# A state-space scan gated by an MLP on one core: 63 tasks in other places of a hand-kept order, 13 small operations on other engines, and the last product kept in PSUM

## The chip, the core and the metric

The kernel runs on one core of one Trainium2 chip. The core has five engines with a queue each, which run in order and wait for one another by semaphores: PE (TensorE, matrix products into PSUM), ACT (ScalarE), DVE (VectorE), POOL (GpSimd) and SP (SyncE, which here issues most of the DMAs). The metric is the device time of one execution in microseconds (us); lower is better. A profile of one execution, with every instruction's start and duration, goes with it.

## The reference

One sequence of 2048 tokens with 448 channels. The normalised input goes through a diagonal complex recurrence (448 states) and, beside it, through an MLP of 1792 hidden units; the product of both is added to the input.

```python
x = A_x
xn = _layernorm(x)
# A: s
Lam_bar = exp(dt * Lam);  B_bar = ((Lam_bar - 1.0) / Lam)[:, None] * Bmat
h_t = Lam_bar * h_{t-1} + B_bar @ xn_t            # for t in 0..2047
s = 2.0 * (h @ Cmat.T).real + xn * Dskip
# B: g
y = _layernorm(xn)
g = silu(gelu(y @ w1 + b1) @ w2 + b2)
return x + s * g
```

## The kernel before

The 2048 tokens are cut into four groups (g = 0 to 3) of 512. A group has two blocks (b) of 128 partitions, and each partition holds two neighbouring tokens (par = 0, 1), so that the recurrence runs over 256 pairs of tokens.

For each group PE does four kinds of work. The first MLP product (`mm1_run`, L801) runs in 14 half-depth tiles that are handled in pairs: the 448 input channels are split over the upper and lower 64 rows of the array, so each pair has a first half (6 matmuls) and a second half (8 matmuls) that ends the sums in two PSUM banks. Behind each second half ACT takes the two banks through a gelu (L805) into `gT`, which frees the banks for a later pair. The second MLP product (`mm2`, L828) has one block of 14 matmuls for each block and parity, into bank 5 or 6; DVE adds the bias and frees the bank (L831, tile o), and ACT, or ACT and DVE together, makes the silu. The products with B (`bu`, L729) go into bank 4 and are copied to `u_sb` in bf16 (L417, by ACT or DVE). The products with C (`ym`, L871, L874, L877) read the states `h_sb`.

Between `bu` and `ym` lies the recurrence (`ssm`). DVE rotates `u_sb` (L744 to L748), scans (L753, L755), ACT rounds the scan's result to bf16 (L417 vs<-s_w, in a copy of 128x1536 and a smaller one in three parts), and DVE rotates back to `h_sb` (L771 to L775).

Once, in the first 70 us, the kernel also makes its tables: the rotations W by sines on ACT (L640) from an angle whose absolute value is taken at L630/L631; the columns of parameters `cw` by many 128x4 operations (L561, L564, L592 and others, each on POOL or DVE); and the matrices CQ, CZ and LB, each row block by a scaled copy into `tmp` (L658 on ACT or L659 on DVE) and a multiply and add on DVE (L661). `M0` is four sums of seven matmuls (L712, the last one L697) with a diagonal added by DVE (L718).

What sets the order: every operation is recorded as a numbered task with what it reads and writes. At the end the tasks are given out in the order of a table of 633 numbers, `ORDER`, and each engine runs its own in that order. A second table, `SECOND`, lists the tasks that run on the second of two engines allowed for them (`small` is POOL or DVE, `copy` ACT or DVE, `combine` ACT or DVE). Waits are added where a task needs another engine's result.

The end of the program is the last `ym` of group 3, cut in columns 0 to 255 and 256 to 447. DVE multiplies each with g (L885) into `t3` in SBUF, the second operation of each (L891, on POOL for the first part and on DVE for the second) adds x, and the result is stored by DMA.

Of the kernel before, what the change touches and what calls it, by code (L numbers as in the profile page):

```python
# [8 lines left out]
ALU = mybir.AluOpType  # L9
# [150 lines left out]


ORDER = [int(k) for k in """
# [17 lines left out]
""".split()]  # L180
SECOND = [int(k) for k in """
45 53 54 61 63 66 69 74 76 83 112 130 133 158 160 162 163 165 177 184 185 187 189 190 220 222 224 226 228 230 238 248 249 258 266 268 331 362 364 365
384 400 401 436 447 468 480 482 487 491 499 501 502 504 510 528 529 609 612 627
""".split()]


# [14 lines left out]
def bass_recurrent_scan__ssm_conv_s5__mixer_channel_mlp__prompt_kernel(  # L201
# [12 lines left out]
    L, D, F = 2048, 448, 1792  # L214
# [5 lines left out]
    with ExitStack() as es:  # L220
# [27 lines left out]
        o_sb = tmp.bitcast(BF)  # L248
# [27 lines left out]
        g_sb = SB("g_sb", [128, 8, D])  # L276
        t3 = SB("t3", [128, 2, D])
# [15 lines left out]
        def dve(fn, reads=(), writes=(), dur=0.2, prio=0):  # L293
            kb.add("dve", fn, reads, writes, dur=dur, lat=0.12, prio=prio)
# [10 lines left out]
        with nc.Block():  # L305
# [513 lines left out]
            def silu_now(g):  # L819
                return bool(9 >> g & 1)  # L820
# [18 lines left out]
            def late(n):  # L839
                return n >= 15  # L840
# [17 lines left out]
            def ym(g, b, par, prio):  # L858
                gx, hb = g % 2, g % 2
                n = (2 * g + b) * 2 + par  # L860
                gs, fb, ob = n % 8, n % 2, b
                k0 = b * 128 + 1 + par
                cm = (CZ, CQ)[par]
                xs = slice(b * 128, (b + 1) * 128)
                off = (2 * g + b) * 256 * D
                last = g == NG - 1 and b == 1

                def part(c0, c1):
                    bk = 7 if g < NG - 1 else (7, 4, 0)[(2 * b + par + (c0 > 0)) % 3]
                    w = c1 - c0  # L870
                    fns = [lambda e, k=k: e.matmul(psum[:, bk, c0:c1], h_sb[:, hb, k, k0:k0 + 128], cm[:, k, c0:c1], start=(k == 0), stop=False)  # L871
                           for k in range(7)]
                    if par == 0:
                        fns += [lambda e, d=d: e.matmul(psum[:, bk, c0:c1], xnT[:, gx, d, xs], M0[:, d, c0:c1], start=False, stop=(d == 3)) for d in range(4)]  # L874
                        du, rk = 2.1, [f"M0{d}" for d in range(4)] + [f"M0{d}d" for d in range(3)] + [f"CZ{k}" for k in range(7)]
                    else:
                        fns[-1] = lambda e: e.matmul(psum[:, bk, c0:c1], h_sb[:, hb, 6, k0:k0 + 128], cm[:, 6, c0:c1], start=False, stop=True)  # L877
                        du, rk = 1.36 * w / D + (0.05 if w < D else 0), [f"CQ{k}" for k in range(7)]
                    pe(fns, [f"h{hb}", f"hh{hb}", f"hp{hb}"] + ([f"xnT{gx}_{b}"] if par == 0 else []) + rk, [f"ps{bk}"], du, prio + c0 / 1e4)
                    y, ky = psum[:, bk, c0:c1], f"ps{bk}"  # L880
                    if par and not late(n):
                        y, ky = xr[:, b, c0:c1], f"xr{b}"
                        dve(lambda e: e.tensor_tensor(xr[:, b, c0:c1], psum[:, bk, c0:c1], xd[:, g % 2 * 2 + b, c0:c1], ALU.add), [f"ps{bk}", f"xd{g % 2 * 2 + b}"] + ([f"CZ{k}" for k in range(7)] if g == 0 else []), [ky])  # L883
                    if silu_now(g):
                        dve(lambda e: e.scalar_tensor_tensor(out=t3[:, fb, c0:c1], in0=y, scalar=2.0, in1=g_sb[:, gs, c0:c1],  # L885
                                                             op0=ALU.mult, op1=ALU.mult), [ky, f"g{gs}"], [f"t3{fb}_{c0}"])
                    else:
                        dve(lambda e: e.tensor_tensor(t3[:, fb, c0:c1], y, g_sb[:, gs, c0:c1], ALU.mult), [ky, f"g{gs}"], [f"t3{fb}_{c0}"])  # L888
                    far = par and late(n)
                    res = xr[:, b, c0:c1] if far else x_all[:, 2 * g + b, par, c0:c1]  # L890
                    add = lambda e: e.tensor_tensor(o_sb[:, ob, par * D + c0:par * D + c1], t3[:, fb, c0:c1], res, ALU.add)  # L891
                    rd = [f"t3{fb}_{c0}", f"t3{fb}_256"] if c0 == 0 and not (last and par) else [f"t3{fb}_{c0}"]
                    rd += [f"xr{b}"] if far else xk(2 * g + b)
                    on = [("dve", add, 0.1 + (0.28, 0.47)[par] * w / D, 0.12), ("pool", add, 0.2 + 1.1 * w / D, 0.15)]
                    if last and par or 1:
                        kb.either(*on, rd, [f"o{ob}_{par}_{c0}"], prio)
                    else:
                        dve(add, rd, [f"o{ob}_{par}_{c0}"], on[0][2], prio)
                    if last:
                        kb.dma("act" if c0 else "sp", dram_ap(out, off + par * D + c0, [[2 * D, 128], [1, w]]), o_sb[:, ob, par * D + c0:par * D + c1], reads=[f"o{ob}_{par}_{c0}"],  # L900
                               writes=[f"out{g}{b}{par}{c0}"], prio=prio, nbytes=256 * w)
                for c0, c1 in ((0, 256), (256, D)) if last and par else ((0, D),):
                    part(c0, c1)
                if par and not last:
                    kb.dma("sp", dram_ap(out, off, [[2 * D, 128], [D, 2], [1, D]]), o_sb[:, ob, :].rearrange("p (r d) -> p r d", r=2),
                           reads=[f"o{ob}_0_0", f"o{ob}_1_0", f"o{ob}_1_256"], writes=[f"out{g}{b}"], prio=prio, nbytes=229376)
# [58 lines left out]
            for step in STEPS.split():  # L965
                k, g, a = step[0], int(step[1]), step[2:]
# [54 lines left out]
```

## Time and profile before

| | before |
|---|---|
| median of 3 runs (lowest to highest) | 153.15 us (153.08 to 153.63) |
| span of the profiled execution | 151.8 us |
| instructions | 2974 |
| DVE busy | 127.6 us (84%) |
| ACT busy | 99.0 us (65%) |
| matmuls | 1127 |
| DMA, HBM read and written | 6.89 MB, 1.84 MB |

The span runs from the first to the last instruction of one profiled execution; the time has some launch and end around it, so it is 1.35 us longer. A row of the timeline gives a start, a duration, the engine, the line of the kernel, the operation and its tiles; rows that follow one another with the same line are merged and counted. In brackets stands how long the engine had been idle, and who ended that. The chain of waits is followed back from the last instruction and says at each moment which work the end was waiting for.

### The profile page before, as it was taken

How to read it: one execution, taken by the hardware profiler on the slowest of the kernel's cores; microseconds unless marked ns; L12 is line 12 of the kernel's file. 1: busy time of each engine (PE TensorE's matmuls, PEld its weight loads, DVE VectorE, ACT ScalarE, POOL GpSimd, SP SyncE). 2: the span in 40 equal slices, each digit the busy share in tenths (PEclk: the TensorE clock that was granted, in tenths of full speed). 3: DMA queues.
4: the chain of work that ended last, by engine and by line, in shares of the span. 5: the costliest groups of instructions: out<-in, count | busy, mean ns of one | idle time of the engine just before them, and what ended most of it. 6: DMA issues, size and time to landing. Idle time of an engine off the chain costs nothing.

```text
span 151.8 us, 2974 instructions
## 1 busy us (share of the span) xinstructions
PE 147.1 (97%) x1127; PEld 86.6 (57%) x1127; DVE 127.6 (84%) x267; ACT 99.0 (65%) x183; POOL 42.1 (28%) x101
## 2 busy tenths in 40 slices
PE   7899999999999999999999999999999999999992
PEld 7785755454566577545444556764454666555551
DVE  2874999999978979999999996379968726999984
ACT  3888996988789559997898610463579834067400
POOL 5376827153020920010456006200072031000201
PEclk9999999999999999999999999999999999999999
DMA  4999999989997300700003032610331001100022
GB/s 116 262 305 390 266 202 138 219 152 133 165 261 180 65 0 0 138 0 4 0 0 63 4 60 45 154 60 4 60 101 23 0 4 57 64 0 0 4 84 98
DMA packets 31236, 14.73 MB, mean 97 GB/s; under 512 B 24752, under 2 KB 30774, under 8 KB 31222
## 3 DMA queue, kind: packets, MB, share of 16 engines
q1 hardware_dynamic: 30912, 14.26, 41.8%
q0 software_dynamic: 160, 0.23, 1.0%
q8 instruction: 9, 0.15, 0.4%
q10 hardware_dynamic: 150, 0.05, 0.1%
q14 instruction: 5, 0.04, 0.1%
HBM read 6.89 MB, written 1.84 MB: 57 GB/s over the span
## 4 chain that ended last, share of the span: by engine, by line
PE 80%; DVE 9%; DMA 4%; SPq 4%; issue 2%
PE psum L828 23%; PE psum L801 22%; PE psum L729 14%; PE psum L871 13%; DMA x_all<-in_A_x_dram 4%; PE psum L874 4%; SPq L84 4%; PE psum L712 3%; DVE xn_sb L499 2%; DVE lnst L399 1%; DVE s_w L628 1%; PE psum L877 1%; DVE o L831 1%; PE psum L697 1%; DVE tmp L891 1%
## 5 line engine op out<-in xcount | busy, mean ns | idle before, releaser
L801 PE MATMUL psum<-xn2T,w_sb 64*128 64x512 bf16 (+1 forms) x462 | 44.6, 345 | 0.3 <-ACT xn2T L417 0.2
L828 PE MATMUL psum<-w_sb,gT 128*128 128x448 bf16 x224 | 44.5, 353 | 0.2 <-DVE o L831 0.2
L805 ACT ACTIVATE gT<-psum,b1f 128x512 bf16<-128x512 f32 (+1 forms) x66 | 35.9, 625 | 10.4 <-PE psum L801 10.2
L801 PEld LDWEIGHTS psum<-xn2T,w_sb 64*128 64x128 bf16 x462 | 24.1, 109 | 19.8 <-ACT gT L805 2.3
L828 PEld LDWEIGHTS psum<-w_sb,gT 128*128 128x128 bf16 x224 | 21.5, 98 | 20.7 <-DVE o L831 0.6
L417 ACT ACTIVATE u_sb<-psum 128x512 bf16<-128x512 f32 (+2 forms) x22 | 10.5, 478 | 23.0 <-PE psum L729 22.7
L729 PE MATMUL psum<-xnT,BT 128*128 128x256 bf16 x196 | 24.0, 273 | 0.0
L729 PEld LDWEIGHTS psum<-xnT,BT 128*128 128x128 bf16 x196 | 18.9, 98 | 5.4 <-issue 1.1
L891 POOL TENSOR_TENSOR tmp<-t,x_all 128x448 bf16<-128x448 bf16 x5 | 5.2, 1032 | 33.1 <-DVE t L888 30.7
L753 DVE TENSOR_TENSOR_SCAN s_w<-dk,vs 128x774 f32<-128x774 f32 x8 | 14.0, 1760 | 0.1
L500 ACT ACTIVATE xn_sb<-x_all,lnw 128x448 bf16<-128x448 bf16 (+2 forms) x21 | 13.0, 662 | 1.2 <-DVE xn_sb L499 1.1
L417 ACT ACTIVATE vs<-s_w 64x256 bf16<-64x256 f32 (+2 forms) x16 | 10.9, 681 | 2.6 <-DVE s_w L753 1.5
L871 PE MATMUL psum<-CZ,h_sb 128*128 128x448 bf16 x56 | 11.9, 352 | 0.0
L871 PE MATMUL psum<-CQ,h_sb 128*128 128x448 bf16 (+2 forms) x54 | 10.5, 332 | 0.0
L399 DVE BATCH_NORM_STATS2 lnst<-x_all 128x6 f32<-128x448 bf16 x12 | 7.1, 617 | 3.4 <-DMA x_all<-in_A_x_dram 3.4
L831 DVE TENSOR_TENSOR o<-psum,b2bc 128x448 f32<-128x448 f32 x16 | 9.7, 614 | 0.2
L871 PEld LDWEIGHTS psum<-CZ,h_sb 128*128 128x128 bf16 x56 | 5.4, 98 | 4.7 <-DVE lnmv L405 0.4
L871 PEld LDWEIGHTS psum<-CQ,h_sb 128*128 128x128 bf16 x54 | 5.1, 98 | 4.0 <-DVE t L885 0.4
L874 PE MATMUL psum<-M,xnT 128*128 128x448 bf16 x32 | 7.4, 352 | 0.0
L480 POOL TENSOR_TENSOR lnw<-lnw,mhalf 128x8 f32<-128x8 f32 x3 | 7.2, 2404 | 0.3
L883 DVE TENSOR_TENSOR Cr<-psum,xd 128x448 f32<-128x448 f32 x7 | 4.3, 620 | 3.5 <-PE psum L877 3.4
L499 DVE TENSOR_SCALAR xn_sb<-x_all,lnw 128x448 bf16<-128x448 bf16 (+2 forms) x19 | 6.9, 396 | 0.0
(160 smaller groups left out, 189.1 us busy)
## 6 DMA issues: line engine op xcount, KB each, us to landing
out_dram<-tmp SPq DMA_DIRECT2D x7, 224.0 KB, 2.0
x_all<-in_A_x_dram SPq DMA_DIRECT2D x3, 448.0 KB, 4.0
w_sb<-in_B_w_dram SPq DMA_DIRECT2D x3, 448.0 KB, 8.4
w_sb<-in_B_w_dram SPq DMA_DIRECT2D x3, 384.0 KB, 4.8
vs<-in_A_C_re_dram SPq DMA_DIRECT2D x1, 392.0 KB, 11.6
Bn<-in_A_B_im_dram SPq DMA_DIRECT2D x1, 336.0 KB, 10.2
Bn<-in_A_B_re_dram SPq DMA_DIRECT2D x1, 336.0 KB, 10.5
vs<-in_A_C_im_dram SPq DMA_DIRECT2D x1, 336.0 KB, 10.8
```

Of the source, the lines that this page charges most:

```text
L399: dve([lambda e, b=b, par=par, q=q: e.bn_stats(lnst[:, q, :], x_all[:, 2 * g + b, par, :])], [f"x{2 * g + b}"] , [f"st{q}"], 0.62, prio)
L417: kb.either(("act", [lambda e, o=o, i=i: e.activation(o, i, ACT.Copy) for o, i in pairs]), ("dve", [lambda e, o=o, i=i: e.tensor_copy(o, i ...
L499: on = [("dve", [lambda e, o=o, i=i: e.tensor_scalar(o, i, rs, nb, op0=ALU.mult, op1=ALU.add) for o, i in parts], 0.4, 0.12), ("act", [lam ...
L500: ("act", [lambda e, o=o, i=i: e.activation(o, i, ACT.Identity, bias=nb, scale=rs) for o, i in parts], 0.75, 0.2)]
L729: fns = [lambda e, r=r, m=m, d=d: e.matmul(psum[:, 4, r * NK:(r + 1) * NK], BT[:, m, d, :], xnT[:, gx, d, :], start=(d == 0), stop=(d == 6 ...
L753: dve(lambda e, so=so, vi=vi: e.tensor_tensor_scan(so, dk[:].rearrange("p i c -> p (i c)"), vi, 0.0, ALU.mult, ALU.add), ["v", "vl", "dk", ...
L801: return lambda e: e.matmul(view(bk[k]), w1_sb[rows, d, fcol(2 * j + k)], rhs[rows, d, :, :], start=not second and n == 0, stop=second and ...
L805: act([lambda e, k=k: e.activation(gT[:, gb, 2 * j + k, :].rearrange("p (r c) -> p r c", r=2)[:, :, cols], view(bk[k]), ACT.Gelu_apprx_tan ...
L828: fns = [lambda e, fi=fi: e.matmul(psum[:, bk, 0:D], gT[:, gb, fi, q * 128:(q + 1) * 128], w2_sb[:, fi, :], start=(fi == 0), stop=(fi == N ...
L831: dve(lambda e: e.tensor_tensor(o2[:, fb, :], psum[:, bk, 0:D], b2bc[:], ALU.add), [f"ps{bk}", "b2bc"], [f"oo{fb}"], 0.62, prio - 76)
L871: fns = [lambda e, k=k: e.matmul(psum[:, bk, c0:c1], h_sb[:, hb, k, k0:k0 + 128], cm[:, k, c0:c1], start=(k == 0), stop=False) for k in ra ...
L874: fns += [lambda e, d=d: e.matmul(psum[:, bk, c0:c1], xnT[:, gx, d, xs], M0[:, d, c0:c1], start=False, stop=(d == 3)) for d in range(4)]
```

## The change

It leaves the computation as it is. First, two tables have other numbers: 63 tasks behind the head stand elsewhere with respect to the others, and 13 operations run on another engine. Of these seven go from POOL to DVE (six operations on parameters of 128x4 or fewer columns, one diagonal of 128x128), one goes from DVE to POOL, three from ACT to DVE (two scaled copies of 128x448 and a cast of `u_sb`), and two from DVE to ACT (the absolute value of the angle, 128x1024, and another cast of `u_sb`). Second, the product L885 of the last 192 columns is written back to its PSUM bank, where L891 reads it; that L891 is fixed to DVE, on which it already was.

```diff
 ORDER = [int(k) for k in """
-0 13 19 47 9 16 18 20 14 1 94 26 17 95 91 27 92 21 15 24 48 4 96 12 108 93 90 109 97 104 103 25 105 99 22 98 49 50 55 5 51 65 106 2 110 100 111 107 29
+47 16 9 0 19 13 14 1 18 17 24 15 20 4 26 12 25 27 94 21 95 91 96 22 48 90 92 108 29 93 97 109 49 30 50 103 104 110 55 99 32 5 105 106 51 98 65 107 100
...
 SECOND = [int(k) for k in """
-45 53 54 61 63 66 69 74 76 83 112 130 133 158 160 162 163 165 177 184 185 187 189 190 220 222 224 226 228 230 238 248 249 258 266 268 331 362 364 365
...
+45 53 54 61 63 66 69 74 78 79 83 85 88 112 130 133 158 159 160 161 162 163 165 184 185 186 187 189 220 222 224 226 228 230 238 244 248 249 258 266 268
...
                     y, ky = psum[:, bk, c0:c1], f"ps{bk}"
+                    tail = bool(last and par and c0 > 0)
+                    t3v = y if tail else t3[:, fb, c0:c1]
...
                     if silu_now(g):
-                        dve(lambda e: e.scalar_tensor_tensor(out=t3[:, fb, c0:c1], in0=y, scalar=2.0, in1=g_sb[:, gs, c0:c1],
-                                                             op0=ALU.mult, op1=ALU.mult), [ky, f"g{gs}"], [f"t3{fb}_{c0}"])
+                        dve(lambda e: e.scalar_tensor_tensor(out=t3v, in0=y, scalar=2.0, in1=g_sb[:, gs, c0:c1],
+                                                             op0=ALU.mult, op1=ALU.mult), [ky, f"g{gs}"], [f"t3{fb}_{c0}"] + [ky] * tail)
...
-                    add = lambda e: e.tensor_tensor(o_sb[:, ob, par * D + c0:par * D + c1], t3[:, fb, c0:c1], res, ALU.add)
+                    add = lambda e: e.tensor_tensor(o_sb[:, ob, par * D + c0:par * D + c1], t3v, res, ALU.add)
...
-                    if last and par or 1:
+                    if tail:
+                        dve(add, rd + [ky], [f"o{ob}_{par}_{c0}"], on[0][2], prio)
+                    else:
                         kb.either(*on, rd, [f"o{ob}_{par}_{c0}"], prio)
-                    else:
-                        dve(add, rd, [f"o{ob}_{par}_{c0}"], on[0][2], prio)
```

Three places of the order follow. The first is on PE, at the end of the first MLP product of group 0 (L801) and the start of the second (L828).

```order
 L801 MATMUL psum<-xn2T,w_sb 128x512 x8
-L801 MATMUL psum<-xn2T,w_sb 128x2x128 x56
-L828 MATMUL psum<-w_sb,gT 128x448 x56
+L801 MATMUL psum<-xn2T,w_sb 128x2x128 x34
+L828 MATMUL psum<-w_sb,gT 128x448 x6
+L801 MATMUL psum<-xn2T,w_sb 128x2x128 x22
+L828 MATMUL psum<-w_sb,gT 128x448 x50
 L801 MATMUL psum<-xn2T,w_sb 128x512 x90
```

Six of the 56 matmuls of L828 now stand between the L801 ones, 22 matmuls before their end.

The second is on DVE, where the first sums o of group 0 are taken out of PSUM. L631 is the absolute value of the angle, L659 and L661 make LB (in Bn). Before:

```order
L631 SCALAR_TENSOR_TENSOR s_w<-s_w 128x4x256
L659 TENSOR_SCALAR tmp<-Bn,cw 128x448
L661 SCALAR_TENSOR_TENSOR Bn<-Bn,cw,tmp 128x448
L561 TENSOR_TENSOR cw<-cw 128x4
L573 RECIPROCAL cw<-cw 128x4
L831 TENSOR_TENSOR o<-psum,b2bc 128x448
L661 SCALAR_TENSOR_TENSOR Bn<-Bn,cw,tmp 128x448
L831 TENSOR_TENSOR o<-psum,b2bc 128x448
L659 TENSOR_SCALAR tmp<-Bn,cw 128x448
L661 SCALAR_TENSOR_TENSOR Bn<-Bn,cw,tmp 128x448
L659 TENSOR_SCALAR tmp<-Bn,cw 128x448 x2
L831 TENSOR_TENSOR o<-psum,b2bc 128x448
```

And in the change:

```order
L659 TENSOR_SCALAR tmp<-Bn,cw 128x448 x2
L661 SCALAR_TENSOR_TENSOR Bn<-Bn,cw,tmp 128x448
L561 TENSOR_TENSOR cw<-cw 128x4
L573 RECIPROCAL cw<-cw 128x4
L831 TENSOR_TENSOR o<-psum,b2bc 128x448
L661 SCALAR_TENSOR_TENSOR Bn<-Bn,cw,tmp 128x448
L831 TENSOR_TENSOR o<-psum,b2bc 128x448
L592 TENSOR_TENSOR cw<-cw,sgn 128x1
L564 TENSOR_SCALAR cw<-cw 128x4
L561 TENSOR_TENSOR cw<-cw 128x4 x2
L831 TENSOR_TENSOR o<-psum,b2bc 128x448
L374 TENSOR_SCALAR dbc<-dbc 128x448
```

L631 is gone (to ACT) and an L659 has come; ahead of the last o four small operations have taken the place of four larger ones.

The third is on ACT, between the last `u_sb` copies of group 1 and the gelus of group 2. vs<-s_w are the two roundings of group 0's scan, L658 the scaled copy for the last row block of CZ. Before:

```order
L417 ACTIVATE u_sb<-psum 128x512
L417 ACTIVATE vs<-s_w 128x3x2x256
L658 ACTIVATE tmp<-Cr,cw 64x448 x2
L835 ACTIVATE th<-o 128x448
L417 ACTIVATE tmp<-psum 64x448
L417 ACTIVATE u_sb<-psum 128x256
L417 ACTIVATE u_sb<-psum 64x256 x2
L761 ACTIVATE s_w<-s_w 64x1
L762 ACTIVATE s_w<-s_w 64x1
L835 ACTIVATE th<-o 128x448
L417 ACTIVATE vs<-s_w 128x256
L417 ACTIVATE vs<-s_w 64x256 x2
```

And in the change:

```order
L835 ACTIVATE th<-o 128x448
L417 ACTIVATE tmp<-psum 64x448
L417 ACTIVATE u_sb<-psum 128x256
L417 ACTIVATE u_sb<-psum 64x256 x2
L761 ACTIVATE s_w<-s_w 64x1
L762 ACTIVATE s_w<-s_w 64x1
L835 ACTIVATE th<-o 128x448
L417 ACTIVATE vs<-s_w 128x256
L417 ACTIVATE vs<-s_w 64x256 x2
L417 ACTIVATE vs<-s_w 128x3x2x256
L658 ACTIVATE tmp<-Cr,cw 64x448 x2
L805 ACTIVATE gT<-psum,b1f 128x512 x12
```

The large rounding and the scaled copy have moved behind all the others; the first gelus of group 2 follow them directly.

Also, on PE, the four M0 sums (L712, L697) now each stand one block of L729 earlier or later among the `bu` and `mm2` blocks of groups 0 and 1, and two `mm2` blocks of group 1 have changed places with them.

More of the change, by code (lines that the diff above doesn't have):

```diff
@@ L162 @@
 ORDER = [int(k) for k in """
[17 rows of a table removed]
[17 rows of a table added]
 """.split()]
 SECOND = [int(k) for k in """
-45 53 54 61 63 66 69 74 76 83 112 130 133 158 160 162 163 165 177 184 185 187 189 190 220 222 224 226 228 230 238 248 249 258 266 268 331 362 364 365
-384 400 401 436 447 468 480 482 487 491 499 501 502 504 510 528 529 609 612 627
+45 53 54 61 63 66 69 74 78 79 83 85 88 112 130 133 158 159 160 161 162 163 165 184 185 186 187 189 220 222 224 226 228 230 238 244 248 249 258 266 268
+326 331 362 364 365 400 401 436 447 468 480 482 487 491 499 501 502 504 510 528 529 609 612 627
 """.split()]
```

32 rows, old and new, of the table ORDER are left out of this document.

## The prediction

> **What bounds the kernel now.** I read the busy times first, then the chain of waits, then PE's own waits, then the timeline of each engine at the places where the order changes.
>
> ```profile
> span 151.8 us, 2974 instructions
> ...
> PE 147.1 (97%) x1127; PEld 86.6 (57%) x1127; DVE 127.6 (84%) x267; ACT 99.0 (65%) x183; POOL 42.1 (28%) x101
> ...
> PE 80%; DVE 9%; DMA 4%; SPq 4%; issue 2%
> ...
> PEld psum L801 <- ACT gT L805: 2.3, 7, 0.5
> ```
>
> PE is busy for all but 4.7 us, and the chain is PE alone from 27 us to 148 us. The change neither adds nor removes a matmul. So it can win only where PE now waits, and it loses wherever another engine hands PE something later than PE asks for it. The waits that are left are short: the weight loads of the first MLP product (L801) wait for the gelu of ACT (L805) for 2.3 us in all. The profiled execution has a span of 151.8 us; the median of the runs is 153.15, that is 1.35 more, and I add these 1.35 at the end.
>
> Behind 92 us PE, ACT and POOL have the order that they had, and DVE one xd (L848) more; two operands change at the very end. The sum is therefore made of places before 92 us and the tail.
>
> **The head: six matmuls put between (gain 0.3).**
>
> ```profile
> 15.34:16.88 1.54, 1.54 (x31) 1.37 (x28) 1.50 (x6) 1.54 (x4) 1.28 (x4) 1.00 1.10 295
> 16.88:19.03 2.15, 2.02 (x32) 1.29 (x29) 2.01 (x10) 2.15 (x5) 1.90 (x8) 1.00 1.21 232
> ...
> 50.71 2.65 PE psum L828 x14
> ...
> 64.88 2.75 PE psum L828 x14
> ```
>
> These are two neighbouring stretches of PE with the same work by the table, 28 matmuls of L801 each. The first takes 1.54 us, the second 2.15: there each second half stands right behind its own first half and waits for it, as no other work is left to put between. The change puts six matmuls of the second product (L828, 2.65/14 = 0.19 each) there and turns the last first half ahead of the other second half. Crossing between L801 (64 rows) and L828 (128 rows) costs 0.10: a block of 14 takes 2.65 where 128-row work follows and 2.75 where L801 does. One crossing is in the 2.15 already, so the waits are 0.61 - 0.10 = 0.51; two new crossings give back 0.20. Gain 0.3, between 0 (the waits stay) and 0.5.
>
> **The first o (gain 0.35).**
>
> ```profile
> 19.03 8.12 PE L828 MATMUL psum<-w_sb,gT 128*128 128x448 bf16 x42
> ...
> 27.33 2.82 PE L828 MATMUL psum<-w_sb,gT 128*128 128x448 bf16 x14 [0.18 <-DVE o L831]
> ...
> 24.29 1.23 DVE L631 SCALAR_TENSOR_TENSOR s_w<-s_w 128x1024 f32<-128x1024 f32 x1
> 25.44 0.44 DVE L659 TENSOR_SCALAR tmp<-Bn,cw 128x448 f32<-128x448 bf16 x1
> ...
> 26.68 0.59 DVE L831 TENSOR_TENSOR o<-psum,b2bc 128x448 f32<-128x448 f32 x1
> ```
>
> Three blocks of 2.65 from 19.03 would end at 26.98; the fourth starts at 27.33, because o is taken out of its bank at 26.68 only. The change moves L631 (1.15 to the next start) to ACT and takes one L659 (0.44) in its place, so this o comes 0.7 earlier and PE finds the bank free: gain 0.35. On ACT the absolute value costs about what its neighbour of the same shape costs:
>
> ```profile
> L640 ACT ACTIVATE WT<-s_w,sgn 128x1024 bf16<-128x1024 f32 x1 | 1.2, 1151 | 0.0
> ...
> 24.01 0.67 ACT L658 ACTIVATE tmp<-Bn,cw 128x448 f32<-128x448 bf16 x1
> 25.55 1.72 ACT L640 ACTIVATE WT<-s_w 128x768 bf16<-128x768 f32 x2 [0.87 <-DVE s_w L631]
> ...
> 30.26 0.62 DVE L831 TENSOR_TENSOR o<-psum,b2bc 128x448 f32<-128x448 f32 x1
> ...
> 30.91 0.58 ACT L833 ACTIVATE g_sb<-o 128x448 bf16<-128x448 f32 x1 [0.59 <-DVE o L831]
> ```
>
> It starts at 24.3 (its input is ready at 24.25), ends at 25.45, and the sines start where they did, at 25.5: ACT loses its 0.67 and its 0.87 of idle time, and nothing behind is later. The last silu waits for the o of 30.26, which follows PE; so the gelus of the second group start about 0.65 earlier too, and the gain of 0.65 reaches 44 us whole.
>
> **The small operations (nothing, if a hole on DVE is covered).** Of the 13, ten go to DVE and three leave it. Seven of the ten come from POOL, where they are dear, and are tiny on DVE; three come from ACT (two L659, a cast of u_sb):
>
> ```profile
> L561 POOL TENSOR_TENSOR cw<-cw 128x4 f32<-128x4 f32 x10 | 3.3, 340 | 4.9 <-DVE cw L564 3.0 <-DVE cw L573 0.9 <-DVE cw L561 0.8
> ...
> L561 DVE TENSOR_TENSOR cw<-cw 128x4 f32<-128x4 f32 x3 | 0.5, 153 | 0.0
> ...
> L417 DVE CAST u_sb<-psum 128x512 bf16<-128x512 f32 x1 | 0.7, 691 | 0.1
> ...
> 43.25 0.63 DVE L399 BATCH_NORM_STATS2 lnst<-x_all 128x6 f32<-128x448 bf16 x1 [1.12 <-DMA x_all<-in_A_x_dram]
> ...
> 46.96 0.68 DVE L661 SCALAR_TENSOR_TENSOR CQ<-Cr,cw,tmp 128x448 bf16<-128x448 bf16 x1
> ```
>
> A start-to-start place on DVE costs about 0.1, so DVE takes on 7 x 0.1 and two L659 (0.9), and gives away L631 (1.15) and one L561 (0.15): about +0.3; a second cast of u_sb goes to ACT for the one that comes. But the order has a hole: the o of 30.26 now stands ahead of four large operations (1.9 us), right behind the small ones, which end near 28.0, and PE ends its block near 29.5. DVE stands still for some 1.5 us. It is late for the rest up to 43, where it waited 1.12 for x; that wait, and the statistics and normalisations that now stand behind the last CQ, give it back. Adding the rows in the new order from 30.2 on, the last CQ ends near 46.3; PE asks for it at 44.45 + 2.65 - 0.65 = 46.45 (the block below), since the change puts the first M0 block (L712) ahead of an L729 block. So this costs 0; if DVE is later by 0.7, PE is too. The cast of u_sb that moves to DVE then stands behind that CQ, statistics and a normalisation (0.53 + 0.30 + 0.61, to 47.7), 0.15 after PE wants its bank. The third M0 sum (L718) comes behind the two scans on DVE, and L697 waits for it: I make it 0.3, between 0 and 0.6. Together +0.45.
>
> ```profile
> 44.45 2.65 PE psum L828 x14
> ...
> 62.96 0.28 DVE L718 TENSOR_TENSOR M<-psum,s_w 128x128 bf16<-128x128 f32 x1
> ```
>
> **The ACT queue ahead of the third group's gelus (loss 0.95).** This is the largest term.
>
> ```profile
> 61.84 1.49 ACT L417 ACTIVATE vs<-s_w 128x1536 bf16<-128x1536 f32 x1 [0.22 <-DVE s_w L753]
> 63.35 1.35 ACT L658 ACTIVATE tmp<-Cr,cw 64x448 f32<-64x448 bf16 x2
> ...
> 65.89 1.17 ACT L417 ACTIVATE u_sb<-psum 128x256 bf16<-128x256 f32 x3
> ...
> 68.01 1.26 ACT L417 ACTIVATE vs<-s_w 128x256 bf16<-128x256 f32 x3
> ...
> 69.94 1.27 ACT L805 ACTIVATE gT<-psum,b1f 128x512 bf16<-128x512 f32 x2 [0.68 <-PE psum L801]
> 71.45 2.42 ACT L805 ACTIVATE gT<-psum,b1f 128x512 bf16<-128x512 f32 x4 [0.24 <-PE psum L801]
> ...
> 67.64 9.86 PE psum L801 x89
> ```
>
> Before, ACT copies the scan (1.49) and makes a product (1.35) at 61.84, while PE is still at L729; after u_sb (65.89) only 3.4 us of copies follow, ACT is free at 69.27, and waits 0.68 for PE. In the change both stand behind those copies, last before the gelus. u_sb cannot start before its L729 block has ended, and then ACT has 1.17 + 0.9 + 1.26 + 1.49 + 1.35 = 6.2 us to do. In the same time PE does one block of L828 (2.75) and the 20 matmuls up to the first gelu's bank (2.3), 5.1 us. The first gelu is 1.3 late with respect to PE. The bank that it frees is needed 42 matmuls in, 0.9 after the gelu's end before: PE waits 0.4. The second gelu follows at once instead of after 0.24 of idle time and its bank had no slack: another 0.55. By then ACT has caught up, as it needs 1.2 for a pair and PE 1.5. Sum 0.95, between 0.4 (the first wait alone) and 1.3 (all the lateness). No lead from the head can hide it: both engines start from the same L729 block. Behind it on DVE stand the products for h (L771 on), 1.7 later than they could be; h was ready at 72.0 and is first asked for at 77.5, so this is covered; uncovered it would cost 1.7.
>
> ```profile
> 71.73 0.29 DVE L775 TENSOR_TENSOR h_sb<-pa 128x256 bf16<-128x256 bf16 x1
> ...
> 77.50 1.43 PE psum L871 x7
> ```
>
> **The tail (gain 0.05).**
>
> ```profile
> 148.87 0.75 POOL L891 TENSOR_TENSOR tmp<-t,Cr 128x256 bf16<-128x256 bf16 x1 [4.90 <-DVE t L885]
> ...
> 149.01 0.35 DVE L885 SCALAR_TENSOR_TENSOR t<-psum,g_sb 128x192 bf16<-128x192 f32 x1
> 149.40 0.44 DVE L891 TENSOR_TENSOR tmp<-t,Cr 128x192 bf16<-128x192 bf16 x1
> ...
> 149.87 0.39 ACTq L84 DMA_DIRECT2D out_dram<-tmp  x1
> ```
>
> The last product is written to PSUM and the last sum reads it there. No row shows a DVE write to PSUM; the nearest is the 0.35 that reads PSUM, and the sum of 0.44 runs while POOL adds 256 columns. I take 0.40 for it and 0.35 for the product, with 0.1 either way. [...]
>
> [...]
>
> **The sum.** -0.30 - 0.35 + 0.45 + 0.95 - 0.05 = +0.7 us. Span 152.5, time 152.5 + 1.35 = 153.85, slower by 0.46%.
>
> **The rivals.**
>
> First, ACT arrives in time and the head's gain stays, which is not slower. It decides if the first gelu is late by under 0.9, the slack of its bank, for instance because the copies run faster when ACT doesn't meet DVE. For it: the gelu before had 0.68 of idle time ahead of it. Against: 6.2 us are seven rows that the trace has. Then -0.65 - 0.05 and between 0 and 0.45: 152.45 to 152.9.
>
> Second, DVE becomes the bound. DVE is at 7.46 of 7.50 us from 61.8 to 69.3 and 14.26 of 14.60 up to 92.
>
> ```profile
> 61.80:69.30 7.50, 7.50 (x52) 3.72 (x52) 7.46 (x17) 7.20 (x14) 0.39 (x1) 1.00 0.32 60
> ...
> 77.40:92.00 14.60, 14.60 (x86) 7.61 (x85) 14.26 (x27) 8.66 (x16) 4.96 (x6) 1.00 0.19 33
> ```
>
> Two holes of about 1.6 are put into it. If the first isn't given back by 46 us, the first M0 block waits 0.7, and if the second isn't by 92, the y products (L871) wait for h and for their bank by another 0.6: 153.85 + 1.3 = 155.15. Against it: the moved sums and statistics take about 0.7 off DVE behind 58 us.
>
> Third, that the insertion doesn't do what it is placed for (its waits merely move to the next pair): 153.85 + 0.3 = 154.15. It lies within the first forecast's range.
>
> **How the numbers follow.** The forecast (ACT's queue costs about one microsecond, third rival included) has 0.55, with 153.3 to 154.6 of its own; the first rival 0.25, the second 0.20. About 0.5%, 0.77 us, is what a measurement of this kernel can tell from no change. Faster than 152.38 needs the first rival at its low end: 0.12. Slower than 153.92 takes a little under half of the forecast and most of the second rival: 0.45. The rest, 0.43, lies between. For 8 in 10 the range reaches from the first rival's 152.4 to the second's 155.15.
>
> **What would show each step.** L828 with six matmuls between the L801 rows near 17.3, and PE from 16.9 to its 28th L801 matmul shorter by 0.3 net; no wait of L828 for the o near 27; DVE standing still before an o near 28; a wait of L697 for L718 near 62; on ACT, the 128x1536 copy and the 64x448 products directly ahead of the gelus, no idle time before the first, and PE's loads of L801 waiting for the gelus twice by about 0.5 between 71 and 74. I am wrong if ACT idles before those gelus, or if a wait over 1 us stands on another engine.

## The result, and the profile after

The changed kernel takes 154.33 us (median of 22 runs, 154.11 to 156.74); the kernel before, run beside it, 153.44 (22 runs, 153.08 to 155.19). The ratio is 1.0066, with a 95% interval of 1.0042 to 1.009: slower by 0.7%, about 0.9 us. The forecast was 153.85, slower by 0.46%, in a range of 152.4 to 155.15. The sign, the places and most prices held; the total is 0.48 us more. Of this, 0.29 is the kernel before itself: its median is 153.15 in the three runs that the prediction had, and 153.44 in the 22 here. Set against the kernel before, the change costs 0.89 by the medians and 1.03 by the shortest runs, where 0.70 was forecast. That one gain of the sum was not there to be won is the main thing found here.

The first fence is the head of the page of the changed kernel (span; busy time, share and instructions of each engine), the second its table of waits (engine and line that wait, for whom: us in all, times, longest).

```profile
span 152.8 us, 2969 instructions
...
PE 148.0 (97%) x1127; PEld 87.1 (57%) x1127; DVE 127.5 (83%) x274; ACT 98.6 (65%) x182; POOL 39.3 (26%) x95
...
PE 69%; DVE 21%; ACT 6%; issue 1%; DVEq 0%
```

```profile
PEld psum L801 <- ACT gT L805: 3.2, 7, 0.8
...
DVE pa L771 <- ACT vs L417: 2.3, 2, 1.9
...
DVE o L831 <- PE psum L828: 1.7, 1, 1.7
```

PE is as busy as before (97%), but the chain, which was PE alone from 27 us on, now passes through DVE (21%) and ACT (6%). The stretch on DVE reaches from the o at 29.94 to the wait of L697 for L718 at 63.24, 33 us almost without a break; the share of a chain is no price, and what PE lost by DVE in it is only the short waits taken apart below (0.21 at L697, 0.10 for a cast). PE's loads of L801 wait 3.2 for the gelus, where it was 2.3. DVE has two holes: 1.7 ahead of an o, 1.9 ahead of the first product for h.

Now the timelines (start, us, engine, line, operation, tiles; in brackets the idle time before and what ended it). ACT from 62 us, then PE over the same place:

```profile
63.22 0.60 ACT L417 ACTIVATE u_sb<-psum 128x512 bf16<-128x512 f32 x1 [0.95 <-PE psum L729]
...
65.09 1.16 ACT L417 ACTIVATE u_sb<-psum 128x256 bf16<-128x256 f32 x3 [0.24 <-PE psum L729]
...
67.20 2.77 ACT L417 ACTIVATE vs<-s_w 128x256 bf16<-128x256 f32 x4
69.99 1.35 ACT L658 ACTIVATE tmp<-Cr,cw 64x448 f32<-64x448 bf16 x2
71.36 3.58 ACT L805 ACTIVATE gT<-psum,b1f 128x512 bf16<-128x512 f32 x6
```

```profile
67.63 4.71 PE L801 MATMUL psum<-xn2T,w_sb 64*128 64x512 bf16 x42
72.69 0.84 PE L801 MATMUL psum<-xn2T,w_sb 64*128 64x512 bf16 x6 [0.34 <-ACT gT L805]
73.84 2.35 PE L801 MATMUL psum<-xn2T,w_sb 64*128 64x512 bf16 x20 [0.32 <-ACT gT L805]
```

From 65.09 on ACT has no gap until the gelus (the 2.77 are three copies of 128x256 and the 128x1536 copy). The first gelu starts at 71.36, 3.73 after PE's first L801 matmul of this group at 67.63; before, it was 69.94 - 67.57 = 2.37. PE stands twice in the same L801 work that ran as one row of 90 matmuls in the kernel before. By the starts of PE's matmuls the two waits cost 0.51 and 0.49.

The head and the tail, in PE's and DVE's timelines of the same profile:

```profile
17.70 1.31 PE L828 MATMUL psum<-w_sb,gT 128*128 128x448 bf16 x6
18.95 1.39 PE L801 MATMUL psum<-xn2T,w_sb 64*128 64x256 bf16 x22
20.27 9.63 PE L828 MATMUL psum<-w_sb,gT 128*128 128x448 bf16 x50
```

```profile
29.94 0.62 DVE L831 TENSOR_TENSOR o<-psum,b2bc 128x448 f32<-128x448 f32 x1 [1.67 <-PE psum L828]
...
150.07 0.36 DVE L887 SCALAR_TENSOR_TENSOR psum<-psum,g_sb 128x192 f32<-128x192 f32 x1
150.47 0.36 DVE L893 TENSOR_TENSOR tmp<-psum,Cr 128x192 bf16<-128x192 f32 x1
```

The six matmuls stand between the halves, and the 50 L828 matmuls behind them run without a stop where there was one before (9.63 in one row). The last product takes 0.36 with PSUM as its output, and the last sum 0.36 instead of 0.44.

This profile is 1.0 longer than that of before, and it starts PE's first L801 matmul 0.4 later (7.25 against 6.85) with every engine's instructions in the same order up to there. So one profile of each kernel can't take the sum apart; the experiments begin with two more of the kernel before and one more of the changed kernel.

### The profile page after: what moved, and what is told of

The parts are those of the page before. It is cut to its first block, busy times and chain, and to the rows that moved or that the text cites. A ratio compares the mean times of both kernels' runs of the same rounds, so it can differ in the third digit from the quotient of the medians.

```text
span 152.8 us, 2969 instructions
## 1 busy us (share of the span) xinstructions
PE 148.0 (97%) x1127; PEld 87.1 (57%) x1127; DVE 127.5 (83%) x274; ACT 98.6 (65%) x182; POOL 39.3 (26%) x95
## 4 chain that ended last, share of the span: by engine, by line
PE 69%; DVE 21%; ACT 6%; issue 1%; DVEq 0%
PE psum L828 21%; PE psum L801 18%; PE psum L871 13%; PE psum L729 8%; PE psum L874 4%; DVE tmp L659 4%; DVE CQ L661 3%; PE psum L422 3%; DVE s_w L753 2%; DVE Bn L661 2%; DVE lnst L399 2%; ACT vs L417 2%; ACT gT L805 2%; DVE CZ L661 2%; DVE o L831 1%; PE psum L460 1%
## 5 line engine op out<-in xcount | busy, mean ns | idle before, releaser
L801 PE MATMUL psum<-xn2T,w_sb 64*128 64x512 bf16 (+1 forms) x462 | 44.6, 345 | 1.0 <-ACT gT L805 0.7
L828 PE MATMUL psum<-w_sb,gT 128*128 128x448 bf16 x224 | 44.5, 353 | 0.0
L801 PEld LDWEIGHTS psum<-xn2T,w_sb 64*128 64x128 bf16 x462 | 24.2, 109 | 20.5 <-ACT gT L805 3.2
L828 PEld LDWEIGHTS psum<-w_sb,gT 128*128 128x128 bf16 x224 | 21.6, 98 | 19.9 <-DVE pa L771 0.4
L729 PE MATMUL psum<-xnT,BT 128*128 128x256 bf16 x196 | 24.0, 273 | 0.1
L729 PEld LDWEIGHTS psum<-xnT,BT 128*128 128x128 bf16 x196 | 18.7, 98 | 6.0 <-issue 1.2
L871 PE MATMUL psum<-CZ,h_sb 128*128 128x448 bf16 x56 | 11.9, 352 | 0.0
L871 PE MATMUL psum<-CQ,h_sb 128*128 128x448 bf16 (+2 forms) x54 | 10.5, 332 | 0.0
L399 DVE BATCH_NORM_STATS2 lnst<-x_all 128x6 f32<-128x448 bf16 x12 | 7.1, 614 | 2.1 <-DMA x_all<-in_A_x_dram 2.1
L871 PEld LDWEIGHTS psum<-CZ,h_sb 128*128 128x128 bf16 x56 | 5.4, 98 | 4.7 <-DVE vs L746 0.4
L871 PEld LDWEIGHTS psum<-CQ,h_sb 128*128 128x128 bf16 x54 | 5.1, 98 | 4.0 <-DVE t L887 0.4
L885 DVE TENSOR_TENSOR Cr<-psum,xd 128x448 f32<-128x448 f32 x7 | 4.3, 620 | 3.4 <-PE psum L877 3.4
L833 ACT ACTIVATE g_sb<-o 128x448 bf16<-128x448 f32 x8 | 4.3, 570 | 2.4 <-DVE o L831 2.4
```

Of the source, the lines that this page charges most:

```text
L399: dve([lambda e, b=b, par=par, q=q: e.bn_stats(lnst[:, q, :], x_all[:, 2 * g + b, par, :])], [f"x{2 * g + b}"] , [f"st{q}"], 0.62, prio)
L729: fns = [lambda e, r=r, m=m, d=d: e.matmul(psum[:, 4, r * NK:(r + 1) * NK], BT[:, m, d, :], xnT[:, gx, d, :], start=(d == 0), stop=(d == 6 ...
L801: return lambda e: e.matmul(view(bk[k]), w1_sb[rows, d, fcol(2 * j + k)], rhs[rows, d, :, :], start=not second and n == 0, stop=second and ...
L828: fns = [lambda e, fi=fi: e.matmul(psum[:, bk, 0:D], gT[:, gb, fi, q * 128:(q + 1) * 128], w2_sb[:, fi, :], start=(fi == 0), stop=(fi == N ...
```

## The experiments

**Second and third profiles.** No edit.

> The kernel before, unchanged, for a second profile of it. Theory (the load of x for the second group lands at other times in other executions): if its first statistics (L399) start before 13 us, the o of 26.68 comes up to 0.6 earlier and the fourth L828 block does not wait; if after, the 0.18 wait is there again. PE's start at 7 us differs from the first profile by up to 0.4. Rival (the order alone sets it): the same rows within 0.05.

> The kernel before, a third profile. Its own time lies 1.7 to 1.8 above its span, as in every other run. Theory: in a run near 153.15 (span 151.4) PE has no wait for the o at 27 us and none for the second weights at 19 us; in a run near 153.5 (span 151.8) one of them is there, 0.2 to 0.4.

> The changed kernel, a second profile. Theory: the two waits of L801 for the gelus, 0.5 each, stand there whatever the loads do, and the waits for the cast, for u and for L718 (0.10, 0.10, 0.21) too; PE's start at 7 us and with it all that follows may be up to 0.4 earlier than in the first profile (span 152.4 to 152.8).

Measured: 154.13 (span 152.4), 153.16 (span 151.4) and 154.32 (span 152.6). In all three the time lies 1.7 to 1.8 above the span, as in every other run here; the 1.35 that stands ahead of the prediction, and in it, sets the span of one execution beside the median of others. From PE's timelines of the second and third profile of before:

```profile
20.05 10.75 PE L828 MATMUL psum<-w_sb,gT 128*128 128x448 bf16 x56 [0.88 <-DMA w_sb<-in_B_w_dram]
```

```profile
19.02 10.77 PE L828 MATMUL psum<-w_sb,gT 128*128 128x448 bf16 x56
...
67.22 9.93 PE L801 MATMUL psum<-xn2T,w_sb 64*128 64x512 bf16 x90
```

And from the timeline of DVE, the first statistics of x for the second group, in the first, second and third profile of before:

```profile
13.58 2.21 DVE L399 BATCH_NORM_STATS2 lnst<-x_all 128x6 f32<-128x448 bf16 x4 [1.95 <-DMA x_all<-in_A_x_dram]
```

```profile
13.23 2.21 DVE L399 BATCH_NORM_STATS2 lnst<-x_all 128x6 f32<-128x448 bf16 x4 [1.85 <-DMA x_all<-in_A_x_dram]
```

```profile
12.34 2.21 DVE L399 BATCH_NORM_STATS2 lnst<-x_all 128x6 f32<-128x448 bf16 x4 [0.72 <-DMA x_all<-in_A_x_dram]
```

The same instruction, released by the same load, starts at 13.58, 13.23 and 12.34. In the third profile, near the shortest time, all 56 L828 matmuls run through: the wait of 0.35 for the first o, which the prediction took away, isn't there. In the second there is another one in its stead, 0.88 for the weights of L828: the load of x lands late there too, at 13.23, but the fourth block, itself 1.0 later, finds its bank free, which the expectation had not seen. A profile of this kernel shows one draw of such waits.

The third profile of before and the second of after have runs of 153.16 and 154.32, each in the shorter half of its kernel's runs, and start PE's first L801 matmul within 0.01 of each other. Starts of PE's blocks in the two:

| place | before | after | after - before | step |
|---|---|---|---|---|
| first L801 matmul | 6.84 | 6.85 | +0.01 | |
| an L801 block near the end of the first group | 16.00 | 16.17 | +0.17 | +0.16, within the first group, where PE's order is unchanged |
| L828 behind the insertion | 22.82 | 22.70 | -0.12 | -0.29, the insertion |
| fourth L828 block | 26.98 | 26.87 | -0.11 | 0.0, the first o |
| L828 of the second group | 43.93 | 43.81 | -0.12 | 0.0 |
| first L801 of the third group | 67.22 | 67.42 | +0.20 | +0.32, the small operations |
| first bank taken again | 71.76 | 72.47 | +0.71 | +0.51, first gelu |
| second bank taken again | 72.42 | 73.63 | +1.21 | +0.50, second gelu |
| last sum (DVE) | 149.06 | 150.26 | +1.20 | 0.0 |

The last sum itself is shorter by 0.08, so to its end it is 1.12; the times differ by 1.16. Without the 0.17 that no step of the change accounts for it is 1.0; that is also the distance of the shortest runs, 154.11 - 153.08. The first profile of the changed kernel doesn't have the 0.17: from PE's first L801 matmul to the last sum it takes 150.47 - 7.25 = 143.22, where the third of before takes 149.06 - 6.84 = 142.22.

**What the ACT queue costs.** In the changed kernel the 64x448 product goes to DVE, into its hole (run a_czdve):

```diff
 ACT  L417 vs<-s_w 128x1536
-ACT  L658 tmp<-Cr,cw 64x448 x2
 ACT  L805 gT 128x512 (gelu)
 DVE  L499 xn_sb
+DVE  L659 tmp<-Cr,cw 64x448 x2
+DVE  L661 CZ<-Cr,cw,tmp
 DVE  L771 pa<-vs,WT
```

> The changed kernel, with one thing undone in the ACT queue ahead of the third group's gelus: the 64x448 scaled copy of the last CZ (L658, 1.35 on ACT) goes to DVE (L659, about 0.9), where DVE stands still from 68.08 to 70.00, and the CZ itself (L661) directly behind it. Theory (the ACT queue costs the time): the first gelu pair starts about 1.3 earlier with respect to PE, the two waits of L801 for L805 (0.51 each) shrink to under 0.1, and the time falls by 0.9, from 154.3 to 153.4. Rival (DVE is the bound and has two holes): the waits for the gelus go, but the time comes back as waits of L871 for h or for its bank before 92 us, and the total falls by less than 0.3.

Measured: 153.51 (153.34 to 155.09, 12 runs), ratio to before 1.002 (0.9985 to 1.0056); 0.8 under the changed kernel by the medians, and 0.77 by the shortest runs. ACT and PE:

```profile
67.05 2.78 ACT L417 ACTIVATE vs<-s_w 128x256 bf16<-128x256 f32 x4
69.86 1.27 ACT L805 ACTIVATE gT<-psum,b1f 128x512 bf16<-128x512 f32 x2
```

```profile
67.48 9.93 PE L801 MATMUL psum<-xn2T,w_sb 64*128 64x512 bf16 x90
...
80.87 1.31 PE L871 MATMUL psum<-CQ,h_sb 128*128 128x448 bf16 x6 [0.28 <-DVE t L887]
```

The first gelu starts 2.38 after PE's first L801, as before the change, and PE's 90 matmuls are one row again: both waits gone, 1.0. A part comes back where the rival said it would, as a wait of L871 for its bank (0.28), since DVE is now the late one; but 0.3, not all.

The other direction, in the kernel before (run b_actlate); on DVE the products for h go behind the copy, with statistics ahead of them:

```diff
 ACT  L417 u_sb<-psum 128x512
-ACT  L417 vs<-s_w 128x1536
-ACT  L658 tmp<-Cr,cw 64x448 x2
 ACT  L835 th; L417 tmp; L417 u_sb x3; L761, L762; L835 th; L417 vs x3
+ACT  L417 vs<-s_w 128x1536
+ACT  L658 tmp<-Cr,cw 64x448 x2
 ACT  L805 gT 128x512 (gelu)
```

> The kernel before, with only this piece of the change: the 128x1536 copy (L417) and the 64x448 products (L658) stand last ahead of the third group's gelus on ACT, and on DVE the products for h (L771 on) behind the copy, with statistics put ahead of them. Theory: ACT has about 2 us more to do after u_sb than PE leaves it, the gelus come late, L801 waits twice, 0.9 + 0.5; the time rises by 1.4 to 1.7, to about 155. Rival (the order on ACT is not what costs, but the order of PE's blocks or DVE): under 0.4 more than before.

Measured: 155.58 (155.19 to 156.69, 4 runs), ratio 1.013 (1.0062 to 1.0197); the shortest run is 2.1 above the shortest of before, more than the 1.4 to 1.7 expected.

```profile
67.94 4.71 PE L801 MATMUL psum<-xn2T,w_sb 64*128 64x512 bf16 x42
73.45 0.84 PE L801 MATMUL psum<-xn2T,w_sb 64*128 64x512 bf16 x6 [0.80 <-ACT gT L805]
74.60 4.72 PE L801 MATMUL psum<-xn2T,w_sb 64*128 64x512 bf16 x42 [0.32 <-ACT gT L805]
...
82.98 1.31 PE L871 MATMUL psum<-CQ,h_sb 128*128 128x448 bf16 x6 [0.48 <-DVE t L885]
```

Against the third profile of before the first bank comes 0.97 and the second 0.49 later, 1.46 as expected; the 0.54 that L871 then waits for DVE were not in the expectation. (This execution, a run of 155.79, also waits 0.52 near 47 us for the load of BT, which the shortest run need not have.) The late copies on ACT, with the order on DVE that goes with them, make the loss; the place of PE's blocks isn't needed for it. ACT's order without DVE's was not run; the two waits for the gelus are ACT's part, the wait of L871 DVE's.

**The head, together and apart.** In the kernel before, both pieces (run b_head), the first of these diffs alone (b_ins), and the second alone (b_o):

```diff
 PE   L801 last first half of the first group
+PE   L828 x6 (gT 0 to 5)
 PE   L801 the last three half blocks
 PE   L828 x14
-PE   L828 x6 (gT 0 to 5)
 PE   L828 x4, x4, x14, x14
```

```diff
 DVE  L628 ra
-DVE  L631 rb
+DVE  L659 tmp<-Bn,cw
 DVE  L659 tmp<-Bn,cw
 ACT  L833 g_sb
-ACT  L658 tmp<-Bn,cw
+ACT  rb (the absolute value of L631)
 ACT  L640 WT
```

> The kernel before, with only the two pieces at the head: six L828 matmuls between the last first half and the second halves of L801, and L631 on ACT for one L659 that goes to DVE. Theory (head gains 0.65 and keeps it): 28 L801 matmuls and the 20 L828 behind them shorter by 0.3, no wait of L828 for the o near 27, time 153.4 - 0.65 = 152.8 or a little above. Rival (the lead is eaten by the next wait, since ACT or DVE keep their pace behind 44 us): the PE starts are 0.65 earlier at 44 us, but the end is within 0.2 of before.

> The kernel before, with only the six L828 matmuls between the halves of L801; L631 stays on DVE ahead of the first o. Theory (the o's lateness depends on when the load of x for the second group lands on DVE, which differs by up to 1.7 between the profiles taken so far): the 14 L828 matmuls behind start 0.3 earlier, and where that load lands late, near 13.6, PE waits 0.6 for the o and nothing is won at 30 us; where it lands near 12.5, PE waits at most 0.1 to 0.2 and the gain of 0.3 stays. Rival (the o's 0.35 and the insertion's 0.3 are independent): 0.3 whatever the load does.

> The kernel before, with only L631 on ACT and one L659 on DVE for it, ahead of the first o; the six L828 matmuls stay where they were. Theory (the o wait of 0.35 stands in some executions only, those in which the load of x for the second group lands late; the insertion alone made it worse since DVE then waits for the block of 276): the o comes 0.6 to 0.7 earlier and PE waits for it in no execution; the fastest times stay at before's, 153.1 to 153.2, and the median falls by 0.1 to 0.3. Rival (the wait costs 0.35 in every execution): all times fall by 0.35, the fastest to about 152.75.

Measured, with ratios to before: both 153.16 (152.84 to 154.91, 12 runs), 1.0 (0.9962 to 1.0037); the insertion alone 153.76 (153.54 to 155.22, 10 runs), 1.0025 (0.9992 to 1.0059); the first o alone 153.35 (153.14 to 154.47, 12 runs), 0.9995 (0.9971 to 1.002). No interval excludes no change, so I go by the shortest runs (153.09 to 153.12 for the kernel before, run beside them) and by the traces. Both together: 0.27 faster, where 0.65 was expected. The o alone: nothing in the shortest runs, as the theory said, but nothing in the median either (153.35 against 153.34), which should have fallen by 0.1 to 0.3. The insertion alone: 0.45 slower. The traces say the same: from PE's first L801 matmul to the last sum they take 142.22 in the third profile of before, 141.92 with both pieces (148.71 - 6.79), 142.20 with the o alone (149.46 - 7.26) and 142.62 with the insertion alone (149.68 - 7.06). L828 of the first group, with the o alone and with both:

```profile
19.45 10.77 PE L828 MATMUL psum<-w_sb,gT 128*128 128x448 bf16 x56
```

```profile
19.82 9.63 PE L828 MATMUL psum<-w_sb,gT 128*128 128x448 bf16 x50
```

With the o alone the row is as long as in the third profile of before (10.77), which has no wait to take away. The insertion alone loses, and not for the reason that I had given. DVE of that kernel, then its PE:

```profile
23.02 0.63 DVE L831 TENSOR_TENSOR o<-psum,b2bc 128x448 f32<-128x448 f32 x1 [1.03 <-PE psum L828]
...
24.57 1.23 DVE L631 SCALAR_TENSOR_TENSOR s_w<-s_w 128x1024 f32<-128x1024 f32 x1
...
26.96 0.59 DVE L831 TENSOR_TENSOR o<-psum,b2bc 128x448 f32<-128x448 f32 x1
```

```profile
27.61 2.82 PE L828 MATMUL psum<-w_sb,gT 128*128 128x448 bf16 x14 [0.54 <-DVE o L831]
```

Its load of x came early, at 12.99, and the o is late all the same: the six matmuls put the end of the 14-matmul block behind them off by 0.8, DVE stands 1.03 for that block's o, and everything queued behind it, L631 and the next o, comes as much later. So the insertion needs this o earlier on DVE, and with L631 gone (both pieces together) the wait is away; the two edits are one.

**The hole on DVE.** In the changed kernel (run a_nohole) the o is put behind two of the operations it stands ahead of:

```diff
 DVE  L592, L564, L561 x2
-DVE  L831 o
 DVE  L374, L596, L598, L659, L661
+DVE  L831 o
 DVE  L659
```

> The changed kernel, with the o of 29.94 (L831) put behind two of the operations that it stands ahead of (L659, L661), so that DVE's idle time of 1.67 ahead of it goes. Theory (the hole is covered by a wait for x and by statistics that can stand later): DVE is 1.1 earlier to 43 us, CQ is done up to 0.7 earlier, PE's starts do not move by 0.1, time 154.3 as the changed kernel. Rival (DVE is the bound): 0.5 or more faster, 153.8 or less.

Measured: 154.34 (154.12 to 155.0, 4 runs), ratio to before 1.0072 (1.005 to 1.0095): the changed kernel's time to 0.01 by the medians and by the shortest runs (154.12 against 154.11), as the theory said. The profiled run was the 155.0:

```profile
29.04 0.28 DVE L374 TENSOR_SCALAR dbc<-dbc 128x448 bf16<-128x448 bf16 x1 [1.05 <-DMA dbc<-in_A_Dskip_dram]
...
30.45 0.62 DVE L831 TENSOR_TENSOR o<-psum,b2bc 128x448 f32<-128x448 f32 x1
```

DVE waits there for a load, the o is 0.5 later and PE's loads of L801 wait 0.79 for the gelus at 35.60. So in this execution the o pays for what now stands ahead of it, and the hole in the changed kernel kept it free of that. The run doesn't show DVE earlier at 43 us, so that the hole costs nothing is shown by the time alone, of four runs.

**Versions meant to be better than both.** Head and tail on the kernel before (run b_best: both diffs above and the lines of the change for the last 192 columns); the same with one L399 later (b_best3); and the changed kernel with its waits mended (a_best), as in a_czdve and with:

```diff
 b_best3, DVE
-L399 lnst (x of 43 us), ahead of the last three L661
+L399 lnst, behind the last L661 CQ
 a_best
-DVE  L417 u_sb (first group)
+ACT  L417 u_sb (first group)
-ACT  L417 vs 128x1536, behind the three L417 vs 128x256
+ACT  L417 vs 128x1536, behind L417 u_sb x3
-DVE  L718 M, behind L747, L748
+DVE  L718 M, ahead of L747, L748
```

> The kernel before, with the two pieces at the head and the tail (last product and sum in PSUM, its order of the last eleven steps), and nothing of the rest of the change. Theory: the sum of the gains that the change has without its losses, 0.65 + 0.08 = 0.73 below before: about 152.7; the run b_head and this one differ by 0.08. [...]

> The kernel b_best, with one more piece of the change: the statistics of the block of x whose load lands at 43 us (L399) stand behind the last CQ, not ahead of it. Theory: in executions in which that load lands late (44.4 in b_actlate, where the first M0 block waited 0.52) the CQs no longer wait for it; the fastest times stay at 152.8, the spread narrows, median 152.9 to 153.1. Rival (the late load is rare): the same as b_best, 153.15.

> The changed kernel with its waits mended: the last CZ's scaled copy on DVE as in a_czdve (behind the first h product), the 128x1536 copy directly behind u_sb on ACT, the u_sb cast of the first group (L417) back on ACT, the third M0 sum (L718) ahead of L747. Theory: what a_czdve wins (0.8) and the waits for the cast (0.10) and for L718 (0.21) too: 154.3 - 1.1 = 153.2; what a_czdve lost again near 80 us (L871 waits 0.3 for its bank, DVE being late) stays or shrinks to 0: 152.9 to 153.2. Rival (DVE is full between 70 and 90 us): the gain stops at what a_czdve has, 153.5.

Measured: 153.15 (152.78 to 154.35, 12 runs), ratio 0.9971 (0.994 to 1.0001); 153.04 (152.76 to 154.73, 12 runs), 0.9983 (0.9946 to 1.0019); 153.58 (153.02 to 154.84, 12 runs), 1.0018 (0.9994 to 1.0043). By the shortest runs the first two are 0.33 and 0.36 below before, and the head alone 0.27, so the tail gives some 0.06, which is little more than the 0.04 by which the shortest runs of before differ; in its profile the product is again 0.36 and the sum 0.36. The expected 152.7 was missed, since the 0.35 of the first o wasn't there to win. The L399 brought nothing to be seen. The mended change is 1.09 under the changed kernel by the shortest runs, as expected, and level with before. By the medians it is only 0.75 under it and no better than a_czdve (153.58 against 153.51), as the rival said, so that what it wins beyond a_czdve rests on the shortest runs and on the trace: the waits for the cast (0.10 regained) and for L718 (0.12, of an expected 0.21) are shorter there. No version is faster than before beyond its interval; the first is the nearest to it.

## Why the prediction was right, and where it was 0.5 short

**Insertion, -0.30: right in size** (0.29 in the table above), wrong as a separate term: alone it costs 0.45. A gain of 0.29 with two more crossings agrees with the 0.10 each that the trace of before charged, not with 0.25 each, half of the 0.51 of waits, at which the insertion would have won nothing; in the changed kernel the six L828 matmuls take 1.25 from start to start, which is 6 x 0.19 and 0.11 more.

**First o, -0.35: the step that failed.** The wait was read correctly from the one profile of before, and the edit removes it. But that execution was one of the longer ones: its load of x released DVE at 13.58, not 12.34. The profiled run at 153.16 doesn't have the wait, and the edit alone (b_o) changes neither the shortest run nor the median, so the 0.35 was not in the 153.15 from which it was taken. Where the load lands late the edit does what it is there for: in b_best and in the changed kernel it releases DVE at 13.62 and 13.90, and no L828 waits. The same mistake shows in the step "that is 1.35 more, and I add these 1.35 at the end": the distance from span to time is 1.7 to 1.8 in every run, so an execution with a span of 151.8 takes about 153.5, more than that median. 153.15 - 0.30 + 0.45 + 0.95 - 0.05, without the o, is 154.2; from the profiled execution with its own distance 151.8 + 0.7 + 1.7 is 154.2 too. Measured: 154.33; the last 0.1 is of the size by which the medians of before differ from one set of runs to another (153.33 to 153.44). That the load of x is the cause of the wait rests on the profiles; no run moved the load.

**Small operations, +0.45: right in kind, 0.13 too much.** They cost 0.32, from 0.41 of waits and 0.09 won back: 0.10 for the cast on DVE (0.15 predicted), 0.21 for L718 ahead of L697 (0.3 predicted), and 0.10 that I had not named, an L729 block at 54.46 that waits for ACT to empty its bank. The last CQ was done at 46.60 and PE asked for it at 46.67; predicted were 46.3 and 46.45. The hole was covered, with 0.07 to spare.

```profile
45.91 0.69 DVE L661 SCALAR_TENSOR_TENSOR CQ<-Cr,cw,tmp 128x448 bf16<-128x448 bf16 x1
...
47.34 0.68 DVE L417 CAST u_sb<-psum 128x512 bf16<-128x512 f32 x1
...
62.90 0.28 DVE L718 TENSOR_TENSOR M<-psum,s_w 128x128 bf16<-128x128 f32 x1
```

```profile
61.50 1.69 PE L729 MATMUL psum<-xnT,BT 128*128 128x256 bf16 x14
63.24 0.94 PE L697 MATMUL psum<-CQ,Bn 128*64 128x448 bf16 x7
```

L697 starts 1.74 after the block of 14 ahead of it, where such a block takes 1.53 without a wait.

**ACT queue, +0.95: right.** 0.51 and 0.50, predicted 0.4 and 0.55. The recorded terms, 6.2 of ACT against 5.1 of PE, give a lateness of 1.1 and not the 1.3 that was written; the 0.2 between them is the time from the end of the L729 block to the start of the copy (64.89 to 65.09 in the changed kernel), which the text leaves out. Measured are 3.73 - 2.37 = 1.36. Nothing is lost later: the products for h, 1.9 late on DVE, were covered. a_czdve and b_actlate show the cause from both sides.

**Tail, -0.05: right.** 0.08. The 0.40 for a sum that reads PSUM was the author's estimate, between the 0.35 and the 0.44 of the rows of before; no run shows it. Measured, the sum falls from 0.44 to 0.36, and the product goes from 0.35 to 0.36. The sum reads its product from PSUM in f32 where it read it from SBUF in bf16, and POOL is still running when it starts in both kernels (before it starts at 149.40 and POOL ends at 149.62, after at 150.47 and 150.69). Why it is shorter isn't shown: source and type change together, and no run has the sum with POOL at rest.

**The rivals.** ACT in time: no; nor did its copies run faster with DVE out of the way: the 128x1536 copy takes 1.49 at 61.84 in the kernel before, with DVE busy for 1.46 of it, and 1.49 at 68.48 in the changed kernel, with DVE at rest throughout. DVE as the bound: not in the changed kernel, where filling the first hole wins nothing; but its price appears as soon as another change moves the bound (0.28 in a_czdve, 0.48 in b_actlate, both L871 waiting for DVE). Waits that merely move: not with both edits; the insertion alone does lose, by another wait, that of L828 for the o. The forecast of 153.85 came within its range, but its nearness owes something to chance: the 0.35 that wasn't there and the 0.13 too much for the small operations go against each other.

## What to carry to other kernels

Before a wait is counted as a gain, see whether it stands in the executions that make up the median: compare the profiled run's own time (here its span and 1.7 to 1.8) with the others, and ask whether the wait hangs on a load. An engine's queue just ahead of the work that frees the bottleneck's banks is priced by adding its rows from the last event that both engines share; that sum held to 0.1 us here. And an insertion that puts one block's end off puts off all that is queued behind its reader.

## What was not expected of the hardware

The same loads in the same order land at different times in different executions: the first statistics of the second group's x started between 12.2 and 13.9 us in the profiles of these kernels, the weights of L828 were once 0.88 late and the skip vector 1.05. PE's first L801 matmul started between 6.79 and 7.26 although nothing ahead of it was moved. In the profiles of the kernel before, such waits are the whole excess over its shortest span (0.35 in the first, about 1.0 in the second), as much as most single edits of this change are worth; that they make the spread of the runs without a profile isn't shown. Why a load comes late was not tried.

Another part of the spread is the granted clock. In the profile of a_best, a run of 154.84 with a mean of 0.989, it is 0.50 from 7.1 to 9.0 us and 0.68 from there to 11.1, and PE's first 42 L801 matmuls take 4.05, where they take 2.50 in the profiles of before. The runs listed with 0.987 to 0.989 are 1.1 to 2.0 us above the median of their kernel. What brings the clock down was not tried.
